# Spectral mixing and a gated feed-forward network on one core: where the sigmoid writes, when the folds run, and the order of the first chunk and of the tail

## The chip, the cores and the metric

One Trainium2 chip, one of its cores. The metric is the device time of one execution in microseconds (us). The engines are PE (matmuls; PEld are its weight loads), DVE (VectorE), ACT (ScalarE), POOL (GpSimd) and SP (which here only issues transfers). Each engine works through its own instructions in order, and waits on semaphores for the others.

## What is computed

Eight sequences of 3008 rows and 256 features go through a two-dimensional Fourier transform, of which the real part is kept, and then, row by row, through a gated feed-forward network with 1536 hidden features. All is in 32-bit floating point.

```python
X = np.fft.fft(x, axis=1)
X = np.fft.fft(X, axis=2)
y = X.real.astype(np.float32).reshape(B * S, D)     # B, S, D = 8, 3008, 256
gate = 1.0 / (1.0 + np.exp(-(y @ w_gate)))          # 256 x 1536
val = y @ w_val
out = (gate * val @ w_out).astype(np.float32)       # 1536 x 256
```

## The kernel before

**The transforms.** The transform over the features is merged into the weights of gate and value: G1 and G2 hold the cosine and the sine part of the feature transform times `w_gate` and `w_val` (`merge`, four matmuls for each 256 columns, copied from PSUM by ACT, L289 and L290). The transform over the rows is a matmul with tables of cosines and sines. Before it, the rows and features of a sequence are folded onto each other by their symmetry: `fold_ops` makes 24 small operations of a sequence (L318 to L347), on POOL for sequences 1 to 7. The transformed sequence is two arrays, P (`pk`) and Q (`qk`), made by `whole` from the folded x. Because of the symmetry, rows k and S - k come from the same P and Q: one as P + Q, the other as P - Q.

**The main loop.** A sequence is six chunks of 252 row pairs (the last has 246), a chunk is 12 steps, one for each 128 hidden features. There are 576 steps, numbered i; i % 12 is the step in its chunk, and three steps make a group p = i // 3. Sequence b of the transform, counted from 0, is used in chunks 6b to 6b + 5. In step i the PE makes `pf`, a PSUM bank with gate and value side by side:

- `front_a(i)` adds G1 times P to pf (L501, "P part");
- `part(i)` keeps the half-way result as `ae`, on ACT with a factor of 2 (L508), in chunk 0 on the DVE together with an edge term (L511, twice);
- `front_b(i)` adds G2 times Q (L518, "Q part"). It has to wait for ae, since it writes the bank that ae is read from;
- `gate_a(i)`, run one step later, makes the sigmoid of the rows k (L528, ACT), the rows S - k as twice the half-way result minus the sum (z, L533; L530 in chunk 0; DVE) and the product of gate and value for the rows k (h, L534, DVE);
- `gate_b(i)` makes the sigmoid of the rows S - k (L546, ACT), their product (h, L547, DVE), and then on POOL the sums of blocks of h that the output product needs (sf, L552): 7 after the second step of a group, 6 after the third, none after the first.

pf takes its bank from three that turn round; from chunk 1 on ACT first writes an edge term into it (`seed`, L494, two a step).

**The output product.** `back(p, part)` multiplies blocks of h and sf with forms of `w_out` (wf) into five PSUM banks `po`: 15 products of blocks for a group, spread over steps 3p + 5 to 3p + 7. The forms are sums and copies of blocks of `w_out` (`forms`, 11 sums on POOL at L304, four copies on ACT). After the fourth group of a chunk ACT copies the banks into c (L575), and `finish` queues 20 sums on c (L592, DVE, the table `C_SUMS`), four transposes (L599) and the stores. The list `later` releases three of these in each step: they run in steps 4 to 11 of the next chunk. Steps 0 to 3 have none.

**Chunk 0.** Weights arrive as 64-bit floating point and are turned into 32-bit ones while chunk 0 runs: `weight_parts` (L253 and L254, ACT), `weight_join` (L263, L264, L266 on the DVE, an addition on POOL, L268), `weight_load` (SP), `weight_use` (a merge, or forms). In steps 0 to 8 there is one of each. A merge is emitted at the end of its step, after the Q part.

**What else is timed by steps.** `at(i, ...)` puts work at the end of step i: reloads of x, the folds (evenly over some 60 steps for the sequences 3 to 7, over 42 for the first two), the transforms (`whole`, four of them, at step 4 of the fourth chunk of the sequence before, for sequence 1 of the sixth). SP issues the transfers, in the order of the program; those of the small `ge` columns (L292) stand there among the weight loads.

Of the kernel before, what the change touches and what calls it, by code (L numbers as in the profile page):

```python
# [7 lines left out]
F32 = mybir.dt.float32  # L8
I32 = mybir.dt.int32
U32 = mybir.dt.uint32  # L10
AF = mybir.ActivationFunctionType
ALU = mybir.AluOpType
# [52 lines left out]
C_SUMS = (((8, 1, 8, 0), (1, 1, 0, 0), (3, 3, 1, 0), (0, 0, 10, 1), (4, 4, 0, 1), (1, 6, 2, 0),  # L65
# [3 lines left out]
OUT = (3, 12)  # L69
HUGE = float((2 ** 24 - 1 - 2 ** 20) * 2.0 ** -7)  # L70


@with_exitstack
def kernel(
# [10 lines left out]
    nc = tc.nc  # L85
    B, _, _, _, D = xf.shape
    F = moe_w_gate.shape[1]
    P = 128
# [8 lines left out]
    CH = 252  # L97
    NB = 1 + max(b // 3 for b in PLACE)
    WC = 256
    HD = D // 2  # L100
    TB = 32
# [7 lines left out]
    const = ctx.enter_context(tc.tile_pool(name="const", bufs=1))  # L109
# [6 lines left out]
    zp = ctx.enter_context(tc.tile_pool(name="zp", bufs=2))  # L116
# [3 lines left out]
    op = ctx.enter_context(tc.tile_pool(name="op", bufs=1))  # L120
# [55 lines left out]

    x8 = const.tile([NP, B - 1, 4, NQ], F32, name="x8")
    zero = const.tile([2, 1, NO], F32, name="zero")
    tr = dram.tile([P, 2, NQ, NE + NO], F32, name="tr")
    ed = dram.tile([B, NK + 1], F32, name="ed")  # L180

# [90 lines left out]
    def weight_use(j, other=None):  # L272
        w, c = jobs[j]
        if w == 2:
            WO[c] = WS.pop(j)
            for g in range(NG):
                if (3 * g + 2) // 2 == c:
                    forms(g)
        else:
            merge(WS.pop(j), w, c, other)  # L280
# [97 lines left out]
    PQE = {}  # L378
# [92 lines left out]
    H, SF, EK = {}, {}, {}  # L471
# [14 lines left out]
    PF, AP, Z = {}, {}, {}  # L486
# [33 lines left out]
    def gate_a(i):  # L520

        n = cut(i)[2]
        p, fh = i // 3, i % 3
        z = Z[i] = zp.tile([P, 3, CH], F32, name="z", tag="z")[:, :, 0:n]
        if fh == 0:
            H[p] = hp.tile([P, 3, 2 * WC], F32, name="h", tag="h")[:, :, 0 : 2 * n]
        pf, ap = PF.pop(i), AP.pop(i)
        nc.scalar.activation(z[:, 2], pf[:, 0], AF.Sigmoid)  # L528
        if i < NFT:
            nc.vector.scalar_tensor_tensor(out=z[:, 0:2, ::-1], in0=ap, scalar=2.0, in1=pf,  # L530
                                           op0=ALU.mult, op1=ALU.subtract)
        else:
            nc.vector.tensor_tensor(z[:, 0:2, ::-1], ap, pf, op=ALU.subtract)  # L533
        nc.vector.tensor_tensor(H[p][:, fh, 0:n], z[:, 2], pf[:, 1], op=ALU.mult)  # L534

    def block(p, i):

# [3 lines left out]
    def gate_b(i):  # L541

        n = cut(i)[2]
        p, fh = i // 3, i % 3
        z, h = Z.pop(i), H[p]
        nc.scalar.activation(z[:, 0], z[:, 0], AF.Sigmoid)  # L546
        nc.vector.tensor_tensor(h[:, fh, n:], z[:, 0], z[:, 1], op=ALU.mult)  # L547
        if fh == 1:
            SF[p] = sp.tile([P, 6 * WC], F32, name="sf", tag="sf")[:, 0 : 8 * 2 * CH // 3].rearrange(
                "p (s n) -> p s n", s=8)  # L550
        for dst, a, b, op in H_SUMS.get(fh, ()):
            nc.gpsimd.tensor_tensor(block(p, dst), block(p, a), block(p, b),  # L552
                                    op=(ALU.subtract, ALU.add)[op])

    PO = []
    later = []
    C = {}

    def back(p, part):

        b, c, g = groups[p]
        n = chunks[c][1]
        R = 2 * n // 3
        last = p == len(groups) - 1
        if part == 0 and g == 0:
            PO[:] = [pso.tile([P, 2 * WC], F32, name=f"po{t}", tag=f"po{t}") for t in range(NB)]
        for at_, (hb, wb) in list(enumerate(PRODUCTS))[part * 5 : part * 5 + 5]:
            t, j = divmod(PLACE[at_], 3)
            mm(PO[t][:, j * R : (j + 1) * R], wf[:, g, wb], block(p, hb), g == 0 and at_ % 3 == 0,
               g == NG - 1)  # L570
            if g == NG - 1 and at_ % 3 == 2:
                if t == 0:
                    C[0] = cp.tile([P, 10 * WC], F32, name="c", tag="c")
                    nc.gpsimd.memset(C[0][:, 15 * R : 15 * R + 40], 0.0)
                nc.scalar.copy(C[0][:, 3 * t * R : 3 * (t + 1) * R], PO[t][:, 0 : 3 * R])  # L575
        if part == 2:
            del H[p], SF[p]
            if g == NG - 1:
                finish(b, c, last)

    def finish(b, c, last):
        k0, n = chunks[c]
        R = 2 * n // 3
        more = k0 + n > NK
        nb = -(-n // TB)
        t = C.pop(0)
        queues = (nc.sync, nc.scalar) if last else (nc.sync,)
        os_ = []

        def sum_(dst, a, b, op):  # L590
            v = [t[:, i * R : (i + 1) * R] for i in (dst, a, b)]
            nc.vector.tensor_tensor(*v, op=(ALU.subtract, ALU.add)[op])  # L592

        def flip(s, h):
            if not os_:
                os_.append(op.tile([P, NK + 1], F32, name="os", tag="os")[:, 0 : 4 * WC].rearrange(
                    "p (s b h j) -> p s b h j", s=2, h=2, j=TB))
            c0 = OUT[h] * R + (n + more if s else 0)
            nc.vector.transpose(os_[0][:, s, 0:nb, h, :], t[:, c0 : c0 + nb * TB])  # L599

        def store(s):
            m, r0 = (min(n, M - k0), b * S + k0) if s == 0 else (
                n - (k0 == 0) - more, b * S + S - k0 - n + 1 + more)
            full = m // TB
            for a in range(4):
                ps = slice(a * TB, (a + 1) * TB)
                cs = slice(a * 2 * TB, (a + 1) * 2 * TB)
                queues[a % len(queues)].dma_start(
                    out=out[r0 : r0 + full * TB, cs].rearrange("(b t) d -> t b d", t=TB),
                    in_=os_[0][ps, s, 0:full].rearrange("p b h j -> p b (h j)"))  # L610
                if m > full * TB:
                    nc.sync.dma_start(out=out[r0 + full * TB : r0 + m, cs],
                                      in_=os_[0][a * TB : a * TB + m - full * TB, s, full].rearrange(
                                          "p h j -> p (h j)"))

        for h in range(2):
            later.extend([lambda x=x: sum_(*x) for x in C_SUMS[h]])
            later.append(lambda h=h: flip(0, h))
            later.append(lambda h=h: (flip(1, h), h and (store(0), store(1))))
# [3 lines left out]


    nc.gpsimd.memset(zero, 0.0)
    nc.scalar.dma_start(out=dt, in_=dtab.rearrange("(c p) d -> p c d", p=P))
    for j in range(2):
        weight_load(j)
# [31 lines left out]
        weight_round(*js)  # L660
        then()()
    nc.scalar.dma_start(out=ed[0:1], in_=PQE[0][2][0:1])
    nc.scalar.copy(PQE[0][1][0:1, 0:CH], PQE[0][2][0:1, 0:CH])
    for j in range(KEEP, KEEP + 3):
        weight_load(j)
    weight_use(2)
# [4 lines left out]
    def at(i, *fs):  # L671
        side.setdefault(i, []).extend(fs)

    pre = {}
    for j in range(9, len(jobs)):
        pre.setdefault(j - 9, []).append(lambda j=j: weight_parts(j))
        at(j - 9, lambda j=j: weight_join(j))
# [1 line left out]
            at(j - 9, lambda j=j: weight_load(j + 3))  # L681
    for j in range(3, len(jobs)):
        w, c = jobs[j]
        at(2 * c + (-3, -2, 1)[w], lambda j=j: weight_use(j))


    i0 = NFT
# [15 lines left out]
    for b in range(B - 1):  # L703
        s0 = b * per
        g0 = s0 + 3 * i0 + 4 if b else 5 * i0 + 4
        f0, steps = (s0 - 2 * i0, 5 * i0) if b > 1 else (s0 - 4, 42) if b else (i0 + 8, 42)

        def folds(f0, steps, b=b):
            ops = fold_ops(b + 1, 2)
            for i, f in enumerate(ops):  # L710
                at(f0 + i * steps // len(ops), f)
        at(f0 - 1, lambda f0=f0, steps=steps, folds=folds: folds(f0, steps))
        at(g0 - 2, lambda b=b: seq_start(b + 1))
        for blk in (1, 0):
            at(g0, *[lambda b=b, blk=blk, what=what: whole(b + 1, blk, what)() for what in range(2)])
        if b < B - 2:
            at(g0 + 1, lambda b=b: load_x(b + 2))
            for i, f in zip(calm(s0 if b else 3 * i0), mirror_x(b + 2)):
                at(i, f)

    for i in range(count):
        front_a(i)
        if i:
            gate_a(i - 1)
        part(i)
        if i:
            gate_b(i - 1)
        if i >= 5:
            back((i - 5) // 3, (i - 5) % 3)
        front_b(i)  # L730
        for f in pre.pop(i, []):
            f()
        for j in range(max(i0, i + 1), min(count, i + 3)):
            if j not in PF:
                seed(j)
        for f in later[0:3]:
            f()
        del later[0:3]
        for f in side.pop(i, []):
            f()  # L740
# [55 lines left out]
```

## Time and profile before

| | us |
|---|---|
| median of three executions (2020.02 to 2021.75) | 2020.3 |
| the profiled execution | 2022.27 |
| its span, first to last instruction | 2020.5 |
| PE busy with matmuls | 1953.0 |
| POOL busy | 1624.2 |
| DVE busy | 1568.4 |
| ACT busy | 1395.4 |
| first weight load of step 0 | 50.40 |
| first weight load of step 12 (chunk 1) | 120.08 |
| last matmul of the program ends | 2007.32 |

The profile is one execution, recorded instruction by instruction. Its span is 1.8 us shorter than the time of that execution, which is 2.0 us above the median. A name such as "DVE c L592" is an engine, the tile that is written and the line of the kernel. In a line of the timeline come the start in us, the length, the engine, the line, the operation, out<-in, the shape and how many were merged into the line; in square brackets the idle time of the engine before it and what ended it. In a line of waits come the total in us, how often, and the longest. A helper records all matmuls at L125, so they are told apart by their tiles: `pf<-pk` is the P part, `pf<-qk` the Q part, `ps` a merge, `po` the output product, `ev` and `od` the row transform. Each of these is two weight loads and two matmuls in the trace. The granted clock of the PE is 0.993 on average over the span and 0.93 in chunk 0.

### The profile page before, as it was taken

To read this page: it belongs to the slowest core of one execution; us is meant where nothing else is said; L and a number is where in the kernel's file an instruction comes from. 1 tells how busy PE (TensorE), PEld (TensorE's weight loads), DVE (VectorE), ACT (ScalarE), POOL (GpSimd) and SP (SyncE) were. 2 spreads that over 40 slices of the span, in tenths; PEclk is the share of its full clock that TensorE was granted. 3 is DMA by queue.
4 is the path that set the end of the run, shared out by engine and by line. 5 is a ranking of instruction groups with operands and counts; after the bars stand their busy time and mean duration, and the time that the engine had idled before them with its cause. 6 is when DMAs were issued, how large, how long until landed. Compare 5 with 4: busy or idle time off the path is not lost.

```text
span 2020.5 us, 34215 instructions
## 1 busy us (share of the span) xinstructions
PE 1953.0 (97%) x11232; PEld 1792.8 (89%) x11232; DVE 1568.4 (78%) x3065; ACT 1395.4 (69%) x3200; POOL 1624.2 (80%) x2873
## 2 busy tenths in 40 slices
PE   6799999999999999999999999999999999999997
PEld 4689889988999999898999989999899998999997
DVE  7568777886888778876887868788678876777776
ACT  3467666776777767776777767777677776777775
POOL 3699887996889868896889968999588895777775
PEclk8899999999999999999999999999999999999999
DMA  8244413112012120120202120120210010011011
GB/s 262 86 129 87 124 45 107 45 20 80 17 45 49 23 76 14 49 54 21 70 16 75 25 76 16 41 59 15 79 23 14 14 26 14 14 20 20 14 22 23
DMA packets 171413, 101.39 MB, mean 50 GB/s; under 512 B 133860, under 2 KB 163172, under 8 KB 168556
## 3 DMA queue, kind: packets, MB, share of 16 engines
q1 hardware_dynamic: 169410, 98.66, 18.9%
q8 instruction: 88, 1.44, 0.3%
q10 hardware_dynamic: 1824, 0.54, 0.1%
q14 instruction: 91, 0.75, 0.1%
HBM read 74.39 MB, written 50.18 MB: 62 GB/s over the span
## 4 chain that ended last, share of the span: by engine, by line
PE 55%; DVE 30%; ACT 11%; issue 2%; DMA 1%; POOL 0%; DVEq 0%; SPq 0%; ACTq 0%; POOLq 0%
PE pf L125 28%; PE po L125 21%; DVE c L592 17%; DVE z L533 6%; ACT z L546 5%; DVE h L547 5%; PE ev L125 4%; ACT pf L494 2%; ACT ae L508 1%; ACT c L575 1%; DVE os L599 1%; PE ps L125 1%; ACT z L528 1%; PE od L125 1%; DMA x<-in_xf_dram 1%
## 5 line engine op out<-in xcount | busy, mean ns | idle before, releaser
L552 POOL TENSOR_TENSOR sf<-h 128x168 f32<-128x168 f32 (+1 forms) x960 | 537.0, 576 | 274.5 <-DVE h L547 272.3
L552 POOL TENSOR_TENSOR sf<-h,sf 128x168 f32<-128x168 f32 (+1 forms) x1152 | 646.1, 580 | 47.6 <-DVE h L547 47.1
L125 PE MATMUL pf<-qk,G 128*128 128x252 f32 (+1 forms) x2304 | 591.8, 380 | 32.6 <-ACT ae L508 18.4
L125 PE MATMUL pf<-pk,G 128*128 128x252 f32 (+1 forms) x2304 | 582.7, 376 | 0.0
L592 DVE TENSOR_TENSOR c<-c 128x168 f32<-128x168 f32 (+1 forms) x960 | 566.2, 605 | 16.9 <-ACT c L575 3.6
L494 ACT ACTIVATE pf<-ek,ge 128x252 f32<-128x252 f32 (+1 forms) x1128 | 536.0, 475 | 18.5 <-DMA ek<-ed 0.2
L533 DVE TENSOR_TENSOR z<-ae,pf 128x504 f32<-128x504 f32 (+1 forms) x564 | 376.4, 667 | 211.1 <-ACT z L528 210.4
L125 PE MATMUL po<-sf,wf 128*128 128x168 f32 (+1 forms) x3072 | 529.9, 305 | 0.0
L125 PEld LDWEIGHTS pf<-pk,G 128*128 128x128 f32 x2304 | 437.1, 190 | 51.9 <-issue 2.3
L125 PEld LDWEIGHTS po<-sf,wf 128*128 128x128 f32 x3072 | 472.8, 190 | 8.2
L125 PE MATMUL po<-h,wf 128*128 128x168 f32 (+1 forms) x2688 | 475.9, 306 | 3.9 <-POOL wf L304 2.2
L125 PEld LDWEIGHTS pf<-qk,G 128*128 128x128 f32 x2304 | 408.0, 190 | 77.0 <-ACT ae L508 34.6
L125 PEld LDWEIGHTS po<-h,wf 128*128 128x128 f32 x2688 | 427.5, 190 | 21.0 <-POOL wf L304 2.5
L546 ACT ACTIVATE z<-z 128x252 f32<-128x252 f32 (+1 forms) x576 | 236.4, 410 | 275.4 <-DVE z L533 260.2
L508 ACT ACTIVATE ae<-pf 128x504 f32<-128x504 f32 (+1 forms) x564 | 331.2, 587 | 128.3 <-PE pf L125 121.2
L547 DVE TENSOR_TENSOR h<-z 128x252 f32<-128x252 f32 (+1 forms) x576 | 322.7, 560 | 113.1 <-ACT z L546 110.9
L528 ACT ACTIVATE z<-pf 128x252 f32<-128x252 f32 (+1 forms) x576 | 211.7, 368 | 55.0 <-PE pf L125 50.4
L534 DVE TENSOR_TENSOR h<-z,pf 128x252 f32<-128x252 f32 (+1 forms) x576 | 233.4, 405 | 0.0
L575 ACT COPY c<-po 128x504 f32<-128x504 f32 (+1 forms) x240 | 128.2, 575 | 3.9 <-PE po L125 3.1
L552 POOL TENSOR_TENSOR sf<-sf 128x168 f32<-128x168 f32 (+1 forms) x192 | 109.3, 569 | 15.1
L552 POOL TENSOR_TENSOR sf<-sf,h 128x168 f32<-128x168 f32 (+1 forms) x192 | 107.6, 561 | 0.0
L125 PE MATMUL ev<-st,x 63*128 63x376 f32 (+4 forms) x372 | 98.7, 417 | 8.7 <-DVE x L328 8.7
(100 smaller groups left out, 800.8 us busy)
## 6 DMA issues: line engine op xcount, KB each, us to landing
x<-xr SPq DMA_DIRECT2D x14, 1536.0 KB
out_dram<-os SPq DMA_DIRECT2D x380, 56.0 KB
xr<-in_xf_dram SPq DMA_DIRECT2D x14, 768.0 KB
xr<-in_xf_dram SPq DMA_DIRECT2D x35, 256.0 KB
ek<-ed SPq DMA_DIRECT2D x39, 126.0 KB
out_dram<-os SPq DMA_DIRECT2D x288, 7.0 KB
x<-in_xf_dram SPq DMA_DIRECT2D x2, 1512.0 KB
tr<-in_stab_dram SPq DMA_DIRECT2D x2, 1129.5 KB
```

Of the source, the lines that this page charges most:

```text
L125: nc.tensor.matmul(o, l, r, start=start, stop=stop, skip_group_check=True)
L494: nc.scalar.activation(PF[i][:, g], EK[i // NFT], AF.Copy, scale=ge[:, g, f : f + 1])
L508: nc.scalar.activation(AP[i], PF[i], AF.Copy, scale=2.0)
L528: nc.scalar.activation(z[:, 2], pf[:, 0], AF.Sigmoid)
L533: nc.vector.tensor_tensor(z[:, 0:2, ::-1], ap, pf, op=ALU.subtract)
L534: nc.vector.tensor_tensor(H[p][:, fh, 0:n], z[:, 2], pf[:, 1], op=ALU.mult)
L546: nc.scalar.activation(z[:, 0], z[:, 0], AF.Sigmoid)
L547: nc.vector.tensor_tensor(h[:, fh, n:], z[:, 0], z[:, 1], op=ALU.mult)
L552: nc.gpsimd.tensor_tensor(block(p, dst), block(p, a), block(p, b), op=(ALU.subtract, ALU.add)[op])
L575: nc.scalar.copy(C[0][:, 3 * t * R : 3 * (t + 1) * R], PO[t][:, 0 : 3 * R])
L592: nc.vector.tensor_tensor(*v, op=(ALU.subtract, ALU.add)[op])
L599: nc.vector.transpose(os_[0][:, s, 0:nb, h, :], t[:, c0 : c0 + nb * TB])
```

## The change

- `gate_a` writes the sigmoid of the rows k straight into h, where the product is to stand, and the product is made in place, now in `gate_b`. z has two parts instead of three. In chunk 0, where ae is made on the DVE in between, this puts ae ahead of h.
- The fold operations are spread over the steps with i % 12 < 4 alone.
- `weight_use` (merges and forms) runs in the middle of its step, between `gate_b` and `back`, so a merge stands between the P and the Q part. Within a step it now also comes before `weight_join` and `weight_load`.
- A sigmoid of two numbers at the very start has its table loaded there. One row of qk is copied by the DVE instead of ACT.
- The last chunk's tail: the fifth po bank isn't copied; the first sum that needs a block of it reads it from PSUM. Five of the 20 sums run on POOL (`C_LAST`, second number 1). The short stores of the last rows alternate between SP and ACT as the long ones do, and the first half is stored after its own transpose. In `C_SUMS` two sums of every chunk write another block, with the same operands otherwise.

```diff
-           (11, 11, 6, 0), (13, 13, 11, 1)))
+           (6, 11, 6, 0), (13, 13, 6, 1)))
+C_LAST = (((8, 1, 8, 0), 0), ((1, 1, 0, 0), 0), ((3, 3, 1, 0), 0), ((1, 6, 2, 0), 1), ((0, 0, 10, 1), 0),
+          ((11, 0, 11, 0), 1), ((4, 4, 0, 1), 0), ((4, 4, 1, 0), 0), ((11, 11, 5, 0), 1),
+          ((9, 9, 8, 0), 1), ((10, 14, 8, 1), 0), ((7, 7, 10, 0), 0), ((6, 11, 6, 0), 1),
+          ((5, 5, 7, 1), 0), ((9, 13, 9, 1), 0), ((9, 9, 2, 0), 0), ((14, 9, 14, 0), 0),
+          ((13, 13, 6, 1), 0), ((12, 9, 12, 0), 0), ((12, 11, 12, 1), 0))
...
+    table = const.tile([2, 1], F32, name="table")
...
     def gate_a(i):
-        z = Z[i] = zp.tile([P, 3, CH], F32, name="z", tag="z")[:, :, 0:n]
+        z = Z[i] = zp.tile([P, 2, CH], F32, name="z", tag="z")[:, :, 0:n]
...
-        pf, ap = PF.pop(i), AP.pop(i)
-        nc.scalar.activation(z[:, 2], pf[:, 0], AF.Sigmoid)
+        nc.scalar.activation(H[p][:, fh, 0:n], PF[i][:, 0], AF.Sigmoid)
...
-            nc.vector.tensor_tensor(z[:, 0:2, ::-1], ap, pf, op=ALU.subtract)
-        nc.vector.tensor_tensor(H[p][:, fh, 0:n], z[:, 2], pf[:, 1], op=ALU.mult)
+            nc.vector.tensor_tensor(z[:, :, ::-1], AP.pop(i), PF[i], op=ALU.subtract)
...
     def gate_b(i):
+        nc.vector.tensor_tensor(h[:, fh, 0:n], h[:, fh, 0:n], PF.pop(i)[:, 1], op=ALU.mult)
         nc.scalar.activation(z[:, 0], z[:, 0], AF.Sigmoid)
...
     def back(p, part):
-                nc.scalar.copy(C[0][:, 3 * t * R : 3 * (t + 1) * R], PO[t][:, 0 : 3 * R])
+                if not (last and t == NB - 1):
+                    nc.scalar.copy(C[0][:, 3 * t * R : 3 * (t + 1) * R], PO[t][:, 0 : 3 * R])
...
     def finish(b, c, last):
-        def sum_(dst, a, b, op):
-            v = [t[:, i * R : (i + 1) * R] for i in (dst, a, b)]
-            nc.vector.tensor_tensor(*v, op=(ALU.subtract, ALU.add)[op])
+        new = set()
+        def sum_(dst, a, b, op, engine=nc.vector):
+            there = lambda i: last and i >= 3 * (NB - 1) and i not in new
+            v = [PO[NB - 1][:, (i - 3 * NB + 3) * R : (i - 3 * NB + 4) * R] if there(i) else
+                 t[:, i * R : (i + 1) * R] for i in (a, b)]
+            engine.tensor_tensor(t[:, dst * R : (dst + 1) * R], *v, op=(ALU.subtract, ALU.add)[op])
+            new.add(dst)
...
-                    nc.sync.dma_start(out=out[r0 + full * TB : r0 + m, cs],
+                    queues[a % len(queues)].dma_start(out=out[r0 + full * TB : r0 + m, cs],
...
+        if last:
+            for x, e in C_LAST:
+                sum_(*x, engine=(nc.vector, nc.gpsimd)[e])
+                if x[0] == 5:
+                    flip(0, 0)
+                    flip(1, 0)
+            for half in range(2):
+                flip(half, 1)
+                store(half)
+            return
...
     nc.gpsimd.memset(zero, 0.0)
+    nc.scalar.activation(table, zero[:, 0, 0:1], AF.Sigmoid)
     nc.scalar.dma_start(out=dt, in_=dtab.rearrange("(c p) d -> p c d", p=P))
...
-    nc.scalar.copy(PQE[0][1][0:1, 0:CH], PQE[0][2][0:1, 0:CH])
+    nc.vector.tensor_copy(PQE[0][1][0:1, 0:CH], PQE[0][2][0:1, 0:CH])
...
-        at(2 * c + (-3, -2, 1)[w], lambda j=j: weight_use(j))
+        use.setdefault(2 * c + (-3, -2, 1)[w], []).append(lambda j=j: weight_use(j))
...
-        f0, steps = (s0 - 2 * i0, 5 * i0) if b > 1 else (s0 - 4, 42) if b else (i0 + 8, 42)
+        slots = [i for i in range(s0 - 2 * i0 if b > 1 else s0 if b else 2 * i0, g0) if i % i0 < 4]
...
             ops = fold_ops(b + 1, 2)
             for i, f in enumerate(ops):
-                at(f0 + i * steps // len(ops), f)
+                at(slots[i * len(slots) // len(ops)], f)
...
         gate_b(i - 1)
+        for f in use.pop(i, []):
+            f()
         if i >= 5:
             back((i - 5) // 3, (i - 5) % 3)
         front_b(i)
```

More of the change, by code (lines that the diff above doesn't have):

```diff
@@ L523, in gate_a @@
         p, fh = i // 3, i % 3
-        z = Z[i] = zp.tile([P, 3, CH], F32, name="z", tag="z")[:, :, 0:n]
+        z = Z[i] = zp.tile([P, 2, CH], F32, name="z", tag="z")[:, :, 0:n]
         if fh == 0:
             H[p] = hp.tile([P, 3, 2 * WC], F32, name="h", tag="h")[:, :, 0 : 2 * n]
-        pf, ap = PF.pop(i), AP.pop(i)
-        nc.scalar.activation(z[:, 2], pf[:, 0], AF.Sigmoid)
+        nc.scalar.activation(H[p][:, fh, 0:n], PF[i][:, 0], AF.Sigmoid)
         if i < NFT:
-            nc.vector.scalar_tensor_tensor(out=z[:, 0:2, ::-1], in0=ap, scalar=2.0, in1=pf,
+            nc.vector.scalar_tensor_tensor(out=z[:, :, ::-1], in0=AP.pop(i), scalar=2.0, in1=PF[i],
                                            op0=ALU.mult, op1=ALU.subtract)
         else:
-            nc.vector.tensor_tensor(z[:, 0:2, ::-1], ap, pf, op=ALU.subtract)
-        nc.vector.tensor_tensor(H[p][:, fh, 0:n], z[:, 2], pf[:, 1], op=ALU.mult)
+            nc.vector.tensor_tensor(z[:, :, ::-1], AP.pop(i), PF[i], op=ALU.subtract)
     def block(p, i):
@@ L672, in at @@
         side.setdefault(i, []).extend(fs)
-    pre = {}
+    pre, use = {}, {}
     for j in range(9, len(jobs)):
@@ L705, with folds @@
         g0 = s0 + 3 * i0 + 4 if b else 5 * i0 + 4
-        f0, steps = (s0 - 2 * i0, 5 * i0) if b > 1 else (s0 - 4, 42) if b else (i0 + 8, 42)
-        def folds(f0, steps, b=b):
+        slots = [i for i in range(s0 - 2 * i0 if b > 1 else s0 if b else 2 * i0, g0) if i % i0 < 4]
+        def folds(slots, b=b):
             ops = fold_ops(b + 1, 2)
             for i, f in enumerate(ops):
-                at(f0 + i * steps // len(ops), f)
-        at(f0 - 1, lambda f0=f0, steps=steps, folds=folds: folds(f0, steps))
+                at(slots[i * len(slots) // len(ops)], f)
+        at(slots[0] - 1, lambda slots=slots, folds=folds: folds(slots))
         at(g0 - 2, lambda b=b: seq_start(b + 1))
```

## The prediction

> **What bounds the kernel now.** I read the engine totals first, then the waits of the PE's weight loads, then busy time by stretch, then the timeline where waits sit.
>
> ```profile
> PE 1953.0 (97%) x11232; PEld 1792.8 (89%) x11232; DVE 1568.4 (78%) x3065; ACT 1395.4 (69%) x3200; POOL 1624.2 (80%) x2873
> ```
>
> The PE bounds the kernel. A step of the main loop is 3.12 us of weight loads and matmuls wherever nothing waits (first loads of steps at 1000.90, 1004.02, 1007.15). So only PE waits, head and tail can be won.
>
> ```profile
> PEld pf L125 <- ACT ae L508: 34.6, 61, 1.1
> PEld pf L125 <- DVE ae L511: 15.3, 10, 3.8
> PEld po L125 <- POOL wf L304: 2.5, 1, 2.5
> ```
>
> Columns: total us, times, longest. The first wait belongs to chunk 1 onwards, the others to chunk 0. By stretch the first is 12.0 us in 125:500, 21.8 in 500:1600, 0.7 in 1600:1900 and nothing later; folds stop near 1650.
>
> ```profile
> 1000.85 2.57 DVE L592 TENSOR_TENSOR c<-c 128x168 f32<-128x168 f32 x3
> 1004.02 0.83 PEld L125 LDWEIGHTS pf<-pk,G 128*128 128x128 f32 x4
> 1006.96 0.67 DVE L533 TENSOR_TENSOR z<-ae,pf 128x504 f32<-128x504 f32 x1
> ...
> 1009.86 0.72 PEld L125 LDWEIGHTS pf<-qk,G 128*128 128x128 f32 x4 [0.32 <-ACT ae L508]
> ```
>
> Three chunk-end sums took 2.57 us beside a fold (L318, 1000.61 to 1002.05); z then began 2.94 us into its step (0.84 in a light step), the ScalarE queue behind it slipped, and the PE waited in the next step. All but a few of these waits sit in steps 9, 11 and 0 of a chunk, at the end of the eight steps (4 to 11) that carry chunk-end sums.
>
> ```profile
> 73.20:118.80 45.60, 38.50 (x178) 32.67 (x177) 29.96 (x58) 20.29 (x59) 43.04 (x71) 0.93 0.27 77
> 371.45:410.94 39.49, 38.30 (x217) 35.38 (x217) 33.85 (x60) 28.32 (x65) 37.99 (x64) 1.00 0.23 56
> 1055.13:1094.31 39.18, 37.93 (x218) 35.22 (x217) 32.67 (x63) 28.13 (x65) 34.72 (x59) 1.00 0.23 58
> 1701.58:1739.08 37.50, 37.50 (x217) 35.34 (x216) 28.57 (x62) 28.68 (x66) 28.43 (x54) 1.00 0.11 18
> ```
>
> Columns: length, then PE, PEld, DVE, ACT, POOL. The last three are chunks: with folds the DVE is busy 4 to 5 us longer for the same work. In chunk 0 (first line) POOL is full.
>
> ```profile
> 56.20 1.28 ACT L528 ACT_TABLE_LOAD   x1
> 69.58 0.83 PEld L125 LDWEIGHTS pf<-pk,G 128*128 128x128 f32 x4
> 70.95 0.68 DVE L530 SCALAR_TENSOR_TENSOR z<-ae,pf 128x504 f32<-128x504 f32 x1 [1.60 <-ACT z L528]
> 71.88 0.86 DVE L511 SCALAR_TENSOR_TENSOR ae<-ek,ge,pf 128x252 f32<-128x252 f32 x2
> 72.79 0.72 PEld L125 LDWEIGHTS pf<-qk,G 128*128 128x128 f32 x4 [2.38 <-DVE ae L511]
> ...
> 118.48 0.87 PEld L125 LDWEIGHTS po<-h,wf 128*128 128x128 f32 x6 [2.49 <-POOL wf L304]
> 2006.29 3.83 DVE L592 TENSOR_TENSOR c<-c 128x164 f32<-128x164 f32 x12 [3.57 <-ACT c L575]
> ```
>
> In chunk 0 the Q part waits for ae, which the DVE does behind z and h; at step 11 the PE waits for POOL's weight forms. The last line is the tail: a sum takes 0.32 us when POOL is quiet.
>
> **What the Trainium skill says.** "Perfetto Trace Analysis", section Identifying the Most-Contended Engine: judge the PE by its weight loads, as matmul ends are modelled. Agrees: the PE row shows only 18.4 us of the 34.6. "SBUF — State Buffer", section SBUF: two separate sides: a DVE operation with two SBUF inputs and a GpSimd operation share a port pair under a lock. Agrees in direction, not in full blocking: L592 takes 0.325 us alone, 0.583 beside L552, 0.85 to 0.92 beside a fold, while L533 and L534, with one PSUM input, stay at 0.67 and 0.40. "PSUM — Partial Sum Buffer", section PSUM bank collisions raise a hardware error: two readers of one bank on different engines get a dependency. Agrees: L533 waits for L528 (210.4 us) although it reads another slot. "ScalarE: Activation LUTs", section What ACT_TABLE_LOAD costs: 1283 ns a load; the trace has 1.28.
>
> **The change, part by part.**
>
> *Sigmoid into h.* One buffer slot less, same instructions and lengths. In the changed order z still waits for the sigmoid, as both read pf; from chunk 1 on the DVE order z, h, h is unchanged. The sigmoid now waits for POOL's reads of the h three groups back, long done. Cost 0, from -2 to +2 (z could start 0.4 us earlier if that wait went).
>
> *Folds into steps 0 to 3.* 24 fold operations a sequence (mean 1.3 us, L318 1.34, L331 1.37, L347 1.10, L326 and L328 together 1.5) go one per step into 24 slots for sequences 3 to 7, and 24 into 16 slots for sequences 1 and 2 (six a chunk). DVE in a heavy step now: 0.67 + 0.40 + 0.56 + 3 sums. At 0.68 to 0.79 a sum (chunk at 1055) that is 3.7 to 4.0 against 3.12; at 0.515 (chunk at 1701) it is 3.2 less some overlap, and nothing waits. After: folds are gone from there, but POOL leaves step 3 behind. Steps 0 to 3 hold 19 sums x 0.54 + 4 folds x 1.3 = 15.5 us against 12.5, so about 3 us of sums (six folds: 5.6) spill into steps 4 and 5. I take 0.58 a sum: 3.4 less overlap, 0.2 too much a step, 1.6 us by step 11, under the 2.1 us (2.94 - 0.84) that cost nothing above. PE side of the spill: sums of step 3 are wanted in step 6, at least 6.6 us after they are done today, so the spill is covered; without that cover it costs its excess each chunk. What is late next: at the transform (step 4 after the last fold) the last fold ends some 19 us after step 0 of its chunk, in the six-fold chunks up to 25, and the PE's second half wants it at about 23.6 (5 x 3.12 + 8 of the first half). I leave 0.1 us of waits in each of 31 chunks, 0.4 in the eight six-fold ones, and 1.5 at each of the first two transforms: 3.1 + 3.2 + 3.0 = 9.3. Gain 34.6 - 9.3 = 25.3, from 12 to 33.
>
> *Chunk 0.* PE waits there sum to 19.3 (1.42, 3.79, 3 x 2.38, 5 x 0.82, 0.33, 2.49). With ae ahead of h (0.41) and the merge (1.70) between P and Q, each wait for ae is covered: z can start 0.88 into a step (as in step 10 now), ae follows at 1.48 and takes 0.86, so it is ready at 2.34, and P (0.83) and merge (1.70) take 2.53; from step 5 on the po matmuls (1.54) come on top. But POOL holds 43.04 us of work in 73.20:118.80, and its third forms end the run. So most waits only gather at step 11. What counts is when POOL's run starts and its idle time. Step 0: the wait of 1.42 goes under the merge. Step 1: no table load (it moves ahead of dt's transfer on the ACT queue, 2 us later, not wanted until 9.2), the ScalarE's merge copies and two L253/L254 end at 55.0, the DVE's three join operations behind them at 56.0, so the first z starts there instead of 57.91; ae ends at 57.5, Q takes 0.76, no merge follows it: step 2 begins at 58.3 instead of 63.89. The copy of one row of qk, 0.40 on ACT, moves to the DVE, which then idles for the PE (1.26 at 51.67): nothing. Step 3 begins about 7 early; POOL, after seven sums (3.2) and one L268 (1.28), starts step 3's sums at 66.8 instead of 73.21, 6.4 early, and 2.1 of its 2.56 idle goes: 8.5. Against it: forms now stand before L268 on POOL in steps 3 and 5, so weight reloads on SP, and the ge transfers queued behind them, come 5 us later; merges of steps 7 and 8 wait, inside POOL's run. From 3 to 12 (19 only if POOL did not bind).
>
> *Tail.* DVE now 20 sums x 0.32 and four transposes, 1.55, 2006.29 to 2014.25. After: five sums on POOL (2.75 us), beside them about 4.7 DVE sums at 0.58, the other ten at 0.325: 6.0 instead of 6.4, two cross-engine waits inside. Reading PSUM: estimated as SBUF, as L534 reads it at 0.40 for 252 columns. Stores: first at 13.95, reuse of a ring 2.2 us later, last SP issue 18.31. Eight each on SP and ACT: 13.5 + 2.2 + 4 x 0.37 = 17.2. Gain 0.4 + 1.1 = 1.5, from -0.5 to 2.5.
>
> Sum: 25.3 + 8.5 + 1.5 = 35.3. The profiled execution took 2022.27 (span 2020.5 and 1.8 around it): 1987.0. The median is 2.0 below it: **1985**.
>
> **Rivals.**
> Spill: POOL's backlog slows the sums to 0.65, half of the 34.6 stays. For: POOL is at 93 to 96% in fold chunks. Against: chunk 1701 has 9 us of POOL idle, room for 4 folds. 17.3 - 3 + 10 = 24.3: 1996.
> Chunk 0 gives nothing, the wait moves to ge transfers or L268: gain 26.8, 1993.5. For: 43 of 45.6 us POOL. Against: its start plainly depends on the steps before.
> Everything goes: 34 + 14 + 2: 1970. For: fold-free chunks wait for nothing.
> The move does not do what it says (waits come from the sums' own load): gain 10, 2010. Against: chunk 1701.
> Slower: POOL becomes the bound of fold chunks. 52 sums at s plus 4 folds x 1.35 exceed 37.5 from s = 0.617 us (0.57 to 0.59 now). At 0.63: 0.7 x 31 chunks + 3.4 x 8 six-fold chunks = 49, less 34.6 of old waits and 10: 2025. It is slower from about 0.627.
>
> **How the numbers follow.** Forecast 0.51 (own range 1977 to 1993), spill 0.16, no head 0.10, everything 0.08, no effect 0.05, slower 0.10. 0.2% (4 us) is about what a measurement of this kernel tells from no change. Faster: 0.51 + 0.16 + 0.10 + 0.08 + 0.03 = 0.88; within: 0.01 + 0.02 = 0.03; slower: 0.08 + 0.01 = 0.09. Range 1972 to 2008: it leaves out most of everything and of slower.
>
> **What would show it.** Right: waits for ACT ae under 10 us; L592 beside no fold; POOL idle near zero in steps 0 to 3; chunk 1 starting 8 us earlier, with one wait of several us for wf at step 11; last store issued about 10 us after the last matmul (11.0 now). Wrong: PE waits for POOL sf or x in fold chunks, L592 still above 0.63, or chunk 1 not earlier.

## The result and the profile after

The changed kernel takes 1995.12 us in the median of 4 runs (1992.17 to 1995.77), the kernel before, timed with it, 2021.03. The ratio is 0.9868, with a 95% interval from 0.9851 to 0.9885: 26 us less, where 35 were forecast (1985). The range from 1972 to 2008 holds it; the narrower range of the forecast itself, 1977 to 1993, does not. The profiled execution took 1994.77, its span 1993.0, 27.5 less than the span before.

The engine totals and the chain of waits of the changed kernel:

```profile
PE 1945.6 (98%) x11232; PEld 1793.0 (90%) x11232; DVE 1538.4 (77%) x3061; ACT 1395.6 (70%) x3198; POOL 1627.1 (82%) x2878
PE 79%; DVE 12%; ACT 5%; POOL 2%; issue 1%; DMA 1%; SPq 0%; POOLq 0%; DVEq 0%; ACTq 0%
```

The DVE lost 30 us of busy time with the same work per chunk (an instruction that is held up by the GpSimd counts as busy; the last section shows how long), and the chain now runs over the PE for 79% of the span. Before, that line gave PE 55% and DVE 30%.

The waits of the PE's weight loads (total us, times, longest):

```profile
PEld pf L131 <- ACT ae L515: 12.5, 36, 1.2
PEld pf L131 <- DVE ae L518: 6.5, 6, 1.7
PEld ps L131 <- POOL wx L275: 5.9, 1, 5.9
PEld po L131 <- POOL wf L311: 5.1, 2, 3.1
```

The wait for the ScalarE's ae, 34.6 us before, is down by 22.1. The DVE's ae of chunk 0 went from 15.3 to 6.5, but one merge now waits 5.9 us for the GpSimd, which no step did before, and the waits for the weight forms went from 2.5 to 5.1.

Busy time by stretch, the same four stretches as before (length; PE, PEld, DVE, ACT, POOL; then granted clock, DMA share and GB/s):

```profile
66.44:112.97 46.53, 33.99 (x163) 29.44 (x161) 29.83 (x58) 19.26 (x53) 41.63 (x71) 0.92 0.30 89
363.23:402.32 39.09, 38.34 (x218) 35.40 (x217) 32.25 (x60) 27.96 (x66) 35.43 (x60) 1.00 0.23 57
1036.91:1074.34 37.43, 37.43 (x218) 35.19 (x217) 30.73 (x59) 27.40 (x64) 33.62 (x57) 1.00 0.24 61
1675.47:1712.97 37.50, 37.50 (x217) 35.34 (x216) 28.72 (x61) 28.77 (x65) 27.96 (x53) 1.00 0.11 18
```

The third line, a chunk with folds, took 39.18 before and now runs at the PE's pace, as the last one without folds does. The second, from step 1 of chunk 7 to step 1 of chunk 8, holds six fold operations issued in four steps, and gained only 0.4. The first is the GpSimd's run in chunk 0, from the gate sums of step 3 to the third group of weight forms: it begins earlier, but it is no shorter than the 45.3 us of before (73.21 to 118.48), and the GpSimd idles 4.9 us in it where it had idled 2.6, nearly all of it after the merge that waits.

Where the 27.5 us went, from the starts of steps: 22.1 in the waits for ae; 2.75 in chunk 0 (from its first step to chunk 1's: 69.68 before, 66.93 after); 1.4 in the tail (last matmul's end to the end of the span: 13.16 and 11.77); 1.34 ahead of step 0, which starts at 49.06, not 50.40. The last can't be put down to the change. In the fourteen executions profiled for this study step 0 starts between 48.88 and 57.29, and one with the head of the kernel before starts it at 49.05. So below, chunk 0 is counted from step 0.

### The profile page after: what moved, and what is told of

Same layout as the page of the kernel before. It is cut to its first block, busy times and chain, and to the rows that moved or that the text cites. A ratio compares the mean times of both kernels' runs of the same rounds, so it can differ in the third digit from the quotient of the medians.

```text
span 1993.0 us, 34353 instructions
## 1 busy us (share of the span) xinstructions
PE 1945.6 (98%) x11232; PEld 1793.0 (90%) x11232; DVE 1538.4 (77%) x3061; ACT 1395.6 (70%) x3198; POOL 1627.1 (82%) x2878
## 4 chain that ended last, share of the span: by engine, by line
PE 79%; DVE 12%; ACT 5%; POOL 2%; issue 1%; DMA 1%; SPq 0%; POOLq 0%; DVEq 0%; ACTq 0%
PE pf L131 40%; PE po L131 33%; DVE c L604 6%; PE ev L131 4%; DVE z L539 3%; DVE h L553 2%; ACT z L552 2%; ACT pf L501 1%; PE od L131 1%; ACT ae L515 1%; DMA x<-in_xf_dram 1%; POOL wf L311 1%; ACT c L582 1%; POOL sf L558 1%; PE ps L131 1%
## 5 line engine op out<-in xcount | busy, mean ns | idle before, releaser
L539 DVE TENSOR_TENSOR z<-ae,pf 128x504 f32<-128x504 f32 (+1 forms) x564 | 376.5, 668 | 221.2 <-ACT h L534 220.5
L604 DVE TENSOR_TENSOR c<-c 128x168 f32<-128x168 f32 (+1 forms) x950 | 520.9, 564 | 16.9 <-ACT c L582 3.6
L131 PEld LDWEIGHTS pf<-qk,G 128*128 128x128 f32 x2304 | 408.3, 190 | 44.8 <-ACT ae L515 12.5
L553 DVE TENSOR_TENSOR h<-z 128x252 f32<-128x252 f32 (+1 forms) x576 | 335.7, 583 | 115.7 <-ACT z L552 114.5
L534 ACT ACTIVATE h<-pf 128x252 f32<-128x252 f32 (+1 forms) x576 | 213.2, 370 | 81.7 <-PE pf L131 68.7
L551 DVE TENSOR_TENSOR h<-h,pf 128x252 f32<-128x252 f32 (+1 forms) x576 | 233.1, 405 | 0.0
L558 POOL TENSOR_TENSOR sf<-sf,h 128x168 f32<-128x168 f32 (+1 forms) x192 | 112.8, 588 | 0.0
```

The source lines that it names most:

```text
L131: nc.tensor.matmul(o, l, r, start=start, stop=stop, skip_group_check=True)
L534: nc.scalar.activation(H[p][:, fh, 0:n], PF[i][:, 0], AF.Sigmoid)
L539: nc.vector.tensor_tensor(z[:, :, ::-1], AP.pop(i), PF[i], op=ALU.subtract)
L551: nc.vector.tensor_tensor(h[:, fh, 0:n], h[:, fh, 0:n], PF.pop(i)[:, 1], op=ALU.mult)
L604: engine.tensor_tensor(t[:, dst * R : (dst + 1) * R], *v, op=(ALU.subtract, ALU.add)[op])
```

## The experiments

**Folds: undone, alone, and on the wrong side.** Three runs price the move and test its reason. First the changed kernel with the old places:

```diff
-        slots = [i for i in range(s0 - 2 * i0 if b > 1 else s0 if b else 2 * i0, g0) if i % i0 < 4]
+        f0, steps = (s0 - 2 * i0, 5 * i0) if b > 1 else (s0 - 4, 42) if b else (i0 + 8, 42)
...
-                at(slots[i * len(slots) // len(ops)], f)
+                at(f0 + i * steps // len(ops), f)
```

> The changed kernel with the folds alone put back to their old steps (one in every 2.5 steps, two thirds of them in steps 4 to 11). Theory: the folds' place is worth the 22.1 us by which the ScalarE ae waits fell (34.6 to 12.5), and the other parts are worth 5.5, so this runs at 2015 to 2018, with 32 to 36 us of ae waits and the VectorE's chunk-end sums again at 0.60 us or more in the mean. Rival (most of the gain is from something else that changed with the order, and the ae waits fell with it): 2000 to 2008, with ae waits clearly under 30.

The second is the kernel before with the opposite edit:

> The kernel before with the folds alone moved to steps 0 to 3. Theory: ae waits 11 to 14 us, time 1997 to 2001 (22 under before). Rival (the parts lean on one another): under half of it, above 2008.

The third puts all folds where the chunk-end sums are:

```diff
-... if i % i0 < 4]
+... if 4 <= i % i0]
```

> The changed kernel with all folds in steps 4 to 11, those with chunk-end sums. Theory (the waits come from folds beside those sums; before, two thirds of the folds stood there and the PE waited 34.6 us for ae): ae waits of 48 to 65 us, time 2029 to 2046. Rival (it is the evenness of the spread that matters, not the side that the folds lie on): 30 to 40 us of waits, time near 2016, as with the old places.

Measured: 2016.34 (ratio to the kernel before 0.9967, 0.9955 to 0.9979), 2001.98 (0.9900, 0.9883 to 0.9917; 1 us above the expected range) and 2036.66 (1.0072, 1.0058 to 1.0086). The two single ratios multiply to 0.9867, and the changed kernel's own is 0.9868: folds and the rest do not lean on one another. The waits for ae and the group of chunk-end sums (count, busy us, mean ns) of the first run, then of the third:

```profile
PEld pf L131 <- ACT ae L515: 34.4, 62, 1.1
...
L604 DVE TENSOR_TENSOR c<-c 128x168 f32<-128x168 f32 (+1 forms) x950 | 564.0, 609 | 16.9 <-ACT c L582 3.6
```

```profile
PEld pf L131 <- ACT ae L515: 55.0, 77, 1.8
...
L604 DVE TENSOR_TENSOR c<-c 128x168 f32<-128x168 f32 (+1 forms) x950 | 583.0, 629 | 16.9 <-ACT c L582 3.6
```

In the changed kernel the group's mean is 564 ns. Adding up, over the whole trace, the time in which a fold runs beside a chunk-end sum gives 25.6 us in the changed kernel, 122.4 with the old places and 168.1 with the folds on the wrong side; the waits are 12.5, 34.4 and 55.0. More of the one gives more of the other, in three doses, and the total of fold work hardly differs (213 to 226 us). The move's reason holds, and it is not the evenness of the spread that matters.

**What is left of the waits.** In chunk 2 of the changed kernel, the GpSimd, and the DVE at the same time:

```profile
168.78 1.91 POOL L558 TENSOR_TENSOR sf<-h,sf 128x168 f32<-128x168 f32 x3
170.65 0.63 POOL L558 TENSOR_TENSOR sf<-sf,h 128x168 f32<-128x168 f32 x1
171.24 0.54 POOL L558 TENSOR_TENSOR sf<-h,sf 128x168 f32<-128x168 f32 x1
171.85 0.54 POOL L558 TENSOR_TENSOR sf<-sf 128x168 f32<-128x168 f32 x1
172.35 1.44 POOL L325 TENSOR_TENSOR x<-x 128x510 f32<-128x510 f32 x1
```

```profile
172.59 2.57 DVE L604 TENSOR_TENSOR c<-c 128x168 f32<-128x168 f32 x3
175.09 0.67 DVE L539 TENSOR_TENSOR z<-ae,pf 128x504 f32<-128x504 f32 x1
```

Step 6 starts at 172.24. The fold was issued in step 3, but the GpSimd takes its work in order and had gate sums ahead of it; so it meets three chunk-end sums, which take 2.57 us, just as before the change. That suggests moving each fold one step earlier still:

```diff
-        slots = [i for i in range(s0 - 2 * i0 if b > 1 else s0 if b else 2 * i0, g0) if i % i0 < 4]
+        slots = [i for i in range(s0 - 2 * i0 - 1 if b > 1 else s0 - 1 if b else 2 * i0 - 1, g0) if (i + 1) % i0 < 4]
```

> The changed kernel with every fold one step earlier: in steps 11, 0, 1, 2 in the place of 0, 1, 2, 3. Theory: the 12.5 us of ae waits that are left come from folds of steps 2 and 3 that the GpSimd, behind its gate sums, reaches only in steps 4 to 6, where chunk-end sums run; a step earlier they no longer do, and 3 to 7 us of waits are left, 6 to 9 us of time gained. Rival (what is left comes from gate sums beside chunk-end sums, whatever the folds do): 11 to 14 us. A fold of step 11 is issued at that step's end and runs in step 0, so it should cost nothing; if it does, step 0 shows it.

Measured: 1987.77 (0.9831, 0.9817 to 0.9845). The waits:

```profile
PEld pf L131 <- ACT ae L515: 6.5, 20, 1.3
```

Half of the rest went, and no wait of another kind came for it. The rival expected 11 to 14. But late folds are not all of it. The time of folds beside chunk-end sums fell only from 25.6 to 18.1 us. And in the changed kernel five chunks (14, 20 and every sixth up to 38, counted from 0) have no fold beside a chunk-end sum, and yet wait 0.62 us each. In chunk 14 gate sums alone stand beside most of the chunk-end sums, which then take 0.55 to 0.67, and z starts 2.65, 2.97 and 3.25 us into steps 6, 7 and 8.

**Chunk 0: the order on the GpSimd.** The new wait, in the timeline of the changed kernel (start, length, engine and line, operation; in brackets the idle time before it and its releaser):

```profile
88.63 1.27 POOL L275 TENSOR_TENSOR wx<-wx 128x512 int32<-128x512 int32 x1
...
89.95 3.06 PEld L131 LDWEIGHTS ps<-wx,dt 128*128 128x128 f32 x8 [5.91 <-POOL wx L275]
...
93.77 0.37 ACT L296 COPY G<-ps 128x256 f32<-128x256 f32 x1 [7.44 <-PE ps L131]
...
95.01 0.43 DVE L270 TENSOR_SCALAR wx<-wx 128x512 f32<-128x512 f32 x1 [7.47 <-ACT wx L260]
...
96.75 1.29 POOL L275 TENSOR_TENSOR wx<-wx 128x512 int32<-128x512 int32 x1 [2.52 <-issue]
```

The merge of step 7 waits for an add that stands behind eleven weight forms. Behind the merge the ScalarE idles 7.4 us, then the DVE, and at last the GpSimd itself. Two runs change the order; in the first only the forms go back to their steps' ends:

```diff
-        use.setdefault(2 * c + (-3, -2, 1)[w], []).append(lambda j=j: weight_use(j))
+        if w == 2:
+            at(2 * c + 1, lambda j=j: weight_use(j))
+        else:
+            use.setdefault(2 * c + (-3, -2, 1)[w], []).append(lambda j=j: weight_use(j))
```

> The changed kernel, in which the weight forms (eleven GpSimd operations each) stand at the end of steps 3, 5, 9 and 11 again, behind the weight join's last add, while the merges stay between the P and the Q part. Theory: the wait of 5.9 us at step 7's merge goes, as the add that it waits for no longer stands behind eleven forms; the GpSimd idles 4.4 us less between 95 and 105, so chunk 1 starts 2 to 4.5 us earlier and the time is 1991 to 1993. Rival (the GpSimd's work sets the end of chunk 0 in any order): chunk 1 starts within 0.7 us of now and the wait at step 11 takes up all that step 7's gives back.

In the second the merges go back too (the `at` line for all w, in the place of the `use` line):

> The changed kernel with merges and forms both at the end of their steps as before; ae ahead of h stays. Theory: the merge no longer covers ae, so steps 2 to 7 each wait 0.3 to 1.0 us for ae again, but step 7 has no 5.9 us wait; the GpSimd's run starts 1 to 3 us later than in the changed kernel and idles less, so chunk 1 starts within 2 us of 116.0 either way. Rival (the place of the merges carries the whole of chunk 0's gain): chunk 1 starts at 118 or later.

Measured: 1996.6 (0.9865, 0.9846 to 0.9885) and 1994.81 (0.9871, 0.9853 to 0.989): neither differs from the changed kernel. With the forms late, step 7 waits no longer, but step 8 does:

```profile
97.52 0.50 PEld L131 LDWEIGHTS ps<-wx,dt 128*128 128x128 f32 x2 [5.61 <-POOL wx L275]
```

With the merges back, the DVE's ae of chunk 0 is waited for 12.1 us, not 6.5 (four of the waits are 2.05, twice what was expected), no merge waits for more than 0.5, and the third forms come latest:

```profile
119.50 0.78 PEld L131 LDWEIGHTS po<-h,wf 128*128 128x128 f32 x3 [4.64 <-POOL wf L311]
```

From the GpSimd's first sum of step 3 to that release are 46.5 us in the changed kernel, 45.6 with forms late, 43.5 with merges back; the last starts it 1.6 us later after step 0, and its GpSimd idles only 0.5 us in the run. Chunk 0 comes to 66.9, 65.0 and 65.6 us (counted from step 0, which started at 57.02 in the last, so that the expected 116.0 and 118 can't be read off the span). Five executions with the changed kernel's own chunk 0 (it and those with other folds or tail) lie between 64.4 and 67.3. The theory of the first run, 1991 to 1993, failed. Its rival holds in the main: the wait only changes its place, in whatever order the GpSimd works. It goes to steps 5 and 8, though, not to step 11 as the rival had it, where the wait stays 3.1. The place of the merges, to which the prediction gave a part, is worth nothing that shows. Of the rest of chunk 0's change, ae ahead of h was not run alone.

**Chunk 0: less work on the GpSimd.** If the GpSimd's work sets the end of chunk 0, work taken from it must count:

```diff
         for i, (a, b, op) in enumerate(W_SUMS):
-            nc.gpsimd.tensor_tensor(f[:, i], block(a), block(b), ...)
+            e = nc.vector if i in (1, 2, 4, 6, 8, 10) else nc.gpsimd
+            e.tensor_tensor(f[:, i], block(a), block(b), ...)
```

> The changed kernel with six of the eleven sums of each group of weight forms on the VectorE, five on the GpSimd. Theory (chunk 0 lasts as long as the GpSimd's run from step 3 to the third forms, 43 to 45 us of work in any order): that run shortens by 5 to 8 us, and chunk 0 (66.9 us from its first step to chunk 1's) falls to 59 to 63. Rival (the VectorE, at 45 us of 67 already, takes up in ae waits what the GpSimd gives back): 65 to 68.

Measured: 1989.01 (0.9833, 0.982 to 0.9846), chunk 0 60.9 us. The waits of step 7 and step 11 are gone, and step 10 waits 2.8 us for ae; two stretches of it (columns as above):

```profile
66.07:74.58 8.51, 4.37 (x17) 3.45 (x16) 8.25 (x16) 3.69 (x9) 7.85 (x13) 0.80 0.23 62
90.94:95.80 4.86, 4.86 (x28) 4.47 (x27) 4.79 (x9) 2.46 (x6) 3.25 (x5) 1.00 0.02 0
```

The first is step 4, now bound by the DVE: six forms beside gate sums stand ahead of the next z, and ae is waited for 4.5 us. The second is step 8, where PE and DVE are both full and the GpSimd has room. That is shown, then: the GpSimd was the bound, and the DVE is the next one.

**Both together.** Earlier folds and six forms on the DVE, and the same with three (1, 2 and 4):

> The changed kernel with both of the things that gained: folds one step earlier, and six of the eleven sums of each group of weight forms on the VectorE. Theory (they act in different places, the one from chunk 1 on, the other inside chunk 0, so they add): 1981 to 1984; ae waits from the ScalarE 6 to 8 us, chunk 0 60 to 62 us. Rival (they meet in chunks 2 and 3, where the first folds begin): 1985 or more.

> The same with three of the eleven sums on the VectorE, not six. Theory: three take at most 1.8 us in a step on the VectorE, so the wait of 4.5 us for ae at step 4 falls below 2.5, but the GpSimd's run is about 4 us shorter, not 8, and step 11 waits for the third forms again: chunk 0 60 to 63 us, time 1981 to 1986, within 2 us of the version with six. Rival (the fewer on the VectorE the better, its ae waits cost more): chunk 0 below 60.

Measured: 1982.75 (0.9794, 0.978 to 0.9808) and 1983.83 (0.98, 0.9785 to 0.9814), chunk 0 60.7 and 61.3 us. The ratios of the two single edits to the changed kernel (0.9831 and 0.9833 over 0.9868) multiply to 0.9927; the first run's is 0.9925. They add. With three the longest wait for ae is still 3.3, not below 2.5; step 7's merge waits 3.6 for the GpSimd again, and step 11 1.9. The version with six beats both kernels: the one before by 41 us, the changed one by 15 (0.75% by the ratios).

**The small parts.** The tail with the twenty sums on the DVE alone:

```diff
-                sum_(*x, engine=(nc.vector, nc.gpsimd)[e])
+                sum_(*x, engine=nc.vector)
```

> The changed kernel with all twenty sums of the last chunk on the VectorE, stores still alternating between two queues. From the last matmul's end to the end of the span: 13.2 us before, 11.8 in the changed kernel. Theory (stores bring 1.1, the GpSimd's sums 0.4): 12.0 to 12.3. Rival (the GpSimd's sums bring it all): 13.0 or more. Other rival (they bring nothing, beside the VectorE's they slow it as much as they take off it): 11.8 or less.

Measured: 12.1 us from the last matmul's end to the end of the span (single run, 1996.72). In the changed kernel the two engines' sums are these:

```profile
1980.18 2.49 DVE L604 TENSOR_TENSOR c<-c 128x164 f32<-128x164 f32 x6 [3.57 <-ACT c L582]
...
1981.38 2.86 POOL L604 TENSOR_TENSOR c<-c 128x164 f32<-128x164 f32 x5 [1.45 <-DVE c L604]
```

Six sums take 2.49 on the DVE there, 0.42 each, and ten take 3.10 in the run without the GpSimd. From first sum to last transpose are 7.96 us before, 7.45 with the DVE alone and sums that read PSUM, 7.11 with the GpSimd. Eleven executions with the new tail end 11.77 to 11.98 after the last matmul, so the GpSimd brings 0.1 to 0.3 and the rest of the edit, queues, order and PSUM reads, about 1.1. By how much each of these, no run tells. Then the sigmoid to a third slot of z:

> The changed kernel with the sigmoid of k written to a third slot of z again, not to h. Theory: nothing changes, since z waits for the sigmoid anyway (both read one PSUM bank), so ae waits stay at 12 to 13 us, z's wait for the ScalarE at 215 to 225 us, and the time from step 0 on within 1.5 us of the changed kernel's, the granted clock of chunk 0 left aside. Rival (the wait of z for the sigmoid was a matter of the shared tile z): z's wait is over 30 us longer here than in the changed kernel, and ae waits rise.

Measured (single run, 1996.98), the VectorE's wait and the PE's:

```profile
DVE z L539 <- ACT z L534: 224.1, 189, 1.7
```

```profile
PEld pf L131 <- ACT ae L515: 14.0, 38, 2.3
```

z waits as long as in the changed kernel (220.5), so the tile that the sigmoid writes is not the reason. What is left is the PSUM bank that both read; no run gave them two banks. The 1.5 us more of ae waits, a little over what was expected, have one place for the most part: step 5 of chunk 3, right after the matmuls for the extra rows (into pe), waits 2.3 us where the changed kernel waits 1.2; the run with folds alone, which keeps the old slot too, shows 2.1 there. Last, the early table load left out:

```diff
-    nc.scalar.activation(table, zero[:, 0, 0:1], AF.Sigmoid)
```

> The changed kernel without the early table load, which then comes with the first sigmoid, in step 1. Theory: step 1 lasts 0.9 to 1.5 us longer than the 4.58 of the changed kernel and everything up to the GpSimd's run starts that much later; the start of step 0 (between 49.05 and 57.02 in the profiles so far) tells nothing. Rival (the ScalarE has room for it in step 1): step 1 within 0.3 us of 4.58.

Measured (single run, 1995.47): step 1 lasts 5.32 in the place of 4.58. That is 0.74, less than expected and not nothing, and the GpSimd's run begins 0.75 later after step 0. At chunk 1 it no longer shows: 66.6 us, within the spread.

## Why the prediction was right, and where it was not

- *What bounds the kernel, and the folds' mechanism: right.* The three doses show it. Of 25.3 us, 22.1 came. The term that was too small is what was left of the waits, 9.3, where 12.5 stayed: the spill was foreseen as gate sums that run late; folds that run late, behind gate sums, beside chunk-end sums, came on top. The chunks that it priced at 0.1 each (31 by its count, 30 by the edit) kept 6.1 us, not 3.1: ten of them 0.6 each, the others nothing. The eight six-fold chunks kept 5.2, not 3.2. The 3.0 at the first two transforms did not come: no step beside them waits for the GpSimd. The last 1.2 are at step 5 of chunk 3, after the matmuls into pe, where 0.8 stood before.
- *How a fold slows a sum: read wrong.* "Agrees in direction, not in full blocking" rests on means of three sums (2.57 us for three is 0.86 each). Taken one by one, the sum that meets a fold lasts until the fold has ended; the last section has the line. The means that it counted with stand all the same.
- *Chunk 0: wrong in its second half.* "POOL's run starts 6.4 earlier" came out as 5.4 from step 0 on (22.81 us after it before, 17.38 now). "And 2.1 of its 2.56 idle goes" failed: the idle time grew to 4.9, since a merge that waits for the GpSimd stops, through ScalarE and DVE, what the GpSimd needs next. The prediction saw that those merges would wait "inside POOL's run" and took it as hidden. The run became 1.3 us longer, not 2.1 shorter. After its end the PE took another 1.4 longer at a lowered clock. 5.43 - 1.26 - 1.42 is the 2.75 measured. The means of several executions differ by as little: 68.8 in two with the old order, 66.1 in five with the new.
- *Tail: right*, 1.4 against 1.5, and split as forecast (0.4 from the GpSimd, 1.1 from the rest). But the 1.1 was counted as stores alone; with all sums on the DVE the stretch from the first sum to the last transpose is 0.5 shorter already, for which it had nothing.
- *Sigmoid into h: right* within its bounds of 2 us either way; by the one run without it, it takes about 1 us of waits away, in one step.
- *Table load: right that it acts, wrong that it lasts.* It moved step 2 by 0.74 us, of which nothing shows at chunk 1.
- *Ahead of step 0: not foreseen*, 1.34 of the 27.5, well inside what this start moves by between executions: luck, not a gain.
- *The rivals.* "Spill" named the right remainder and overrated it (12.5 left, not half of 34.6); "chunk 0 gives nothing" was nearly so for chunk 0, and one of the two places to which it sent the wait, the add of L268 (L275 in the changed kernel), is where the 5.9 us are. The GpSimd did not become the bound of chunks with folds: the third stretch above has it at 33.62 of 37.43.
- *Its signs.* Waits for ae under 10 us (12.5) and chunk 1 starting 8 us earlier (4.1, with 1.34 of it ahead of step 0) did not come; the wait for weight forms at step 11 (3.1) did.

## What to carry to other kernels

Work moved off a busy stretch lands where its engine's queue lets it run, not where it is issued; place it ahead of that engine's own backlog, and look for it in the trace beside the work that it was to leave. Where an engine is full from one point to the next, as the GpSimd in chunk 0, moving waits about changes their names alone: begin its run earlier, or take work from it. And a wait "hidden" inside a full engine's run is hidden only if nothing that this engine needs stands behind it.

## What the runs showed of the hardware

A DVE sum that reads two SBUF tiles is held by a running GpSimd instruction until that one ends. The first of the three sums of chunk 2 of the changed kernel shown above, beside its fold:

```profile
172.59 1.39 DVE L604 TENSOR_TENSOR c<-c 128x168 f32<-128x168 f32 x1
```

The fold runs from 172.35 to 173.79, the sum ends at 173.98, 0.19 us later; alone it takes 0.32. So it goes for every chunk-end sum that starts while a fold has over 0.1 us to run, 113 in the kernel before, 28 in the changed one and 152 with the folds on the wrong side: all end 0.18 to 0.20 us after the fold, however much of the fold was left. Their time over 0.325 us adds up to 85.2, 16.6 and 120.1 us. Gate sums do the same (642 of 677 in the kernel before), but are shorter, mostly 0.54 to 0.63: the chunk-end sums beside them last 0.59 in the median. z, which reads one tile in SBUF and one in PSUM, keeps its 0.64 to 0.68 us beside either. So a fold costs such a sum more than a gate sum does, and the DVE's busy time holds this waiting.

The PE can pay twice for a long wait. In the fourteen executions profiled, chunk 0 and the two steps after it hold 102 waits of weight loads over 0.7 us. None of the 68 up to 2.06 us is followed by a lower clock in the next 3.4 us; of the 23 from 2.38 to 3.8 us, 15 are, at 0.50 to 0.66; of the 11 over 4.5 us, all are. Two executions with the same instructions in chunk 0, the changed kernel and the one with the folds back, over the whole of step 7 and of step 11 (columns as above):

```profile
83.22:96.52 13.30, 7.79 (x27) 6.54 (x26) 5.69 (x12) 2.61 (x7) 10.86 (x19) 0.74 0.17 48
...
108.29:115.99 7.70, 4.81 (x20) 4.26 (x19) 2.26 (x5) 2.49 (x8) 7.62 (x18) 0.78 0.51 174
```

```profile
85.44:96.82 11.38, 6.81 (x28) 5.63 (x27) 4.92 (x10) 2.61 (x6) 10.00 (x17) 0.85 0.18 46
...
108.43:114.71 6.28, 3.39 (x19) 2.96 (x18) 2.27 (x5) 2.50 (x8) 6.20 (x15) 1.00 0.58 193
```

After waits of 3.14 us in both, step 11's matmuls are busy 4.81 us in the one and 3.39 in the other. The Trainium skill, "TensorE: Matmul & The Clock Gate", section Part 1: The HAM clock gate (the "warmup" mystery), gives a reason: the PE's clock falls to half after an idle window of about 3.4 us, and the window runs freely, whenever the work comes. The halved clock and the chance in it agree with the traces; that the PE must idle for 3.4 us does not, as 13 of the 19 waits between 2.38 and 3.4 were enough, with 1.99 to 2.93 us between the matmuls before and after them. In the kernel before, steps 2 and 3 of chunk 0 both waited 2.38 us for ae and had the same matmuls, busy 3.70 us in step 2 and 5.37 in step 3. So a wait of 2.4 us can cost 4, and in these executions an edit that cuts waits from over 2.4 to under 2.06 us can gain more than what it takes off them.

The start of step 0 moves by up to 8 us between executions, more than most edits here are worth. Of the two versions with earlier folds and forms on the DVE, the one with six forms started it at 57.29, the one with three at 49.95. In their first 40 us they moved this much:

```profile
DMA packets 3255, 10.80 MB, mean 270 GB/s; under 512 B 750, under 2 KB 1006, under 8 KB 2652
```

```profile
DMA packets 3667, 12.02 MB, mean 300 GB/s; under 512 B 778, under 2 KB 1034, under 8 KB 3037
```

The two transfers of x, issued at 1.76 us in both, end the DVE's waits at 13.44 and 19.67 us in the one and at 12.21 and 17.69 in the other; later transfers are issued after these, so part of the lower rate follows from the delay. Why x lands later, no run here tells. Small edits were therefore read from step 0 on.
